# Attention and feed-forward blocks on one core: identity on VectorE, pairs of shift cells in two planes, b2 added on VectorE, a new order of instructions

## The chip, the cores and the metric

The program runs on one core of a Trainium2 chip. A core has five engines, each with its own queue that it works off in order: PE (TensorE, matrix products into PSUM), ACT (ScalarE, activation functions), DVE (VectorE), POOL (GpSimd) and SP (SyncE, which here issues all transfers between HBM and SBUF). Engines wait for each other through semaphores. The metric is the time of one execution on the device in microseconds (us), as a median of several runs.

## The reference

Two layers, each an attention block and a feed-forward block with the same weights, on a sequence of 2048 rows of width 512 in bf16; 32 heads of width 16, hidden width 1792.

```python
def _A_ref(x, wqkv, wo):
    qkv = (x @ wqkv).reshape(B, S, 3, H, Dh).transpose(2, 0, 3, 1, 4)
    q, k, v = qkv[0], qkv[1], qkv[2]
    p = softmax(einsum("bhqd,bhkd->bhqk", q, k) * Dh ** -0.5)
    o = einsum("bhqk,bhkd->bhqd", p, v)
    return o.transpose(0, 2, 1, 3).reshape(B, S, D) @ wo

def _B_ref(x, w1, b1, w2, b2):
    return gelu(x @ w1 + b1) @ w2 + b2

x = A_x
for _ in range(2):
    x = x + _A_ref(_layernorm(x), A_wqkv, A_wo)
    x = x + _B_ref(_layernorm(x), B_w1, B_b1, B_w2, B_b2)
```

## The kernel before

**Cells.** Attention is cut into cells. A cell is a 128 x 512 block of scores: 128 keys (a key tile, `kt`) against 512 columns of queries of one pass. There are 4096 cells. A cell's scores come from one matmul (`score`, L1527) into one PSUM bank; four of them with different row groups run side by side on PE. Then the exponential is taken in one of two ways.

*On ACT* (`exps`, L2120): a group of two or three cells in neighbouring banks is read at once and written as bf16 to `pt` (or to a buffer that is lent for the time: `kt`, `q`, `v`, `g`). One product with V per cell and head follows on PE (`pvs`, L2187), in rounds of four matmuls.

*On DVE and POOL, the shift cells* (`dfirst`, L1794; `dchain`, `shift`, L1983 and L1985): one `tensor_scalar` turns a score into the bits of a bf16 number near its exponential (uint16). Adding 32 to these bits three times gives four planes, and the sum of the four, with V scaled by 1, 0.84, 0.71 and 0.59 (`VC`, made by `vcopies`), is a good approximation. So a shift cell has four products on PE instead of one. Two shift cells make a pair; the additions run for both at once, as `int64_add` on POOL or, where the scheduler finds POOL too late, as `tensor_scalar` on DVE (L1985): the first from plane 0 to plane 1, the second from planes 0 and 1 together to planes 2 and 3. Planes lie in `dp` (NPL of them, each for two cells) or in parts of other tensors that are free for a time (`DU`, four planes each: `kt`, `v`). A pair takes one plane when it begins, one more for the first shift and two for the second (`grab`, `may`, `safe`); a plane comes free when its products are done (`drop`). The table `KD` names the key tiles whose cells may be shift cells; what has not been taken as such by the end of a pass goes to ACT (`next_act`).

**Banks.** PSUM has eight banks. Slot 0 of the exponentials has banks 0 to 2, slot 1 has 3 and 4, and from some time on 5 as a third (`grow`); bank 6 collects the products, bank 7, and 5 before `grow`, serve projections, feed-forward tiles and single shift cells. When a group of scores is issued, its third bank is given to a shift cell if a cell, planes and DVE's queue allow it (`trade`), else to a third cell of ACT (`more`).

**The other work.** Layer norm statistics, projections, output projection and feed-forward tiles are put between the groups of scores; weights come through four ring buffers. `init` makes the constants: a 128 x 128 identity (`IDENT`), of which the head mask (`MASK`) is a sum, rows of ones and zeros, and `B2row`, with b2 in row 0 and zeros in the others. `loads` issues the first transfers. In `ytile` the second feed-forward matmul collects 14 rounds into a bank, then a round of `ONES1` (ones in row 0) by `B2row` adds b2, and DVE adds the bank to x (L1265). In the last chunk of the last layer (four tiles) b2's round comes first. `ln` and `ln_tile` make the layer norms, the first of them behind the mask in DVE's queue. While PE would have nothing to do, it is given fillers, matmuls whose result is not used (`fill`, L1515).

**The order.** When the program is built, `_Sched` plays all threads of work against a model of the engines (costs in us at each operation, latencies, DMA tails) and so fixes the order of every queue; on the chip only semaphores count. Weights of the choices (`NAMES`, `ROWS`) change 100 times along the way, by `PIECES`.

Of the kernel before, what the change touches and what calls it, by code (L numbers as in the profile page):

```python
# [27 lines left out]
QP_RING = 3  # L28
# [5 lines left out]
XLN_RING = 4  # L34
# [12 lines left out]
NPL = 16  # L47
# [21 lines left out]
TAIL = 10  # L69
OPENING = 18  # L70
# [46 lines left out]
)  # L117
PIECES = (24, 31, 1, 10, 32, 1, 27, 27, 23, 26, 4, 5, 25, 31, 27, 29, 32, 19, 11, 28, 10, 18, 8, 13, 11, 13, 23, 13, 30, 23, 11, 9, 10, 29,
          28, 10, 16, 20, 16, 19, 14, 23, 22, 26, 31, 28, 2, 32, 8, 15, 28, 13, 28, 25, 25, 21, 13, 27, 3, 9, 29, 17, 31, 32, 28, 0, 31, 6,
          17, 31, 25, 12, 23, 28, 27, 7, 32, 22, 23, 25, 22, 9, 31, 32, 24, 32, 25, 6, 29, 30, 27, 8, 8, 11, 29, 19, 23, 25, 11, 9)  # L120
# [10 lines left out]
TTAIL = 3.2  # L131
# [7 lines left out]
SPC = 1.5  # L139
# [10 lines left out]
EARLYP = 1  # L150
# [7 lines left out]
VPER = 0.036  # L158
# [11 lines left out]
PORTS = ("OTT", "NMR", "RSTD", "RA.", "RY.", "XLN", "VC", "QP")  # L170
# [137 lines left out]
class _Sched:  # L308
# [169 lines left out]
    def run(self):  # L478
        while True:
# [71 lines left out]
            if e == "pool":  # L551
                self.pool_ops.append((start, start + cost))
# [7 lines left out]
def bass_interleave_layers__mha_block__dense_activation_gelu__prompt_kernel(  # L560
# [15 lines left out]
    with ExitStack() as es:  # L576
# [35 lines left out]
        T["DU"] += deep  # L612
        T["VC"] = sb([128, 2, 3, NKD, H // 4 * 17 + 2], BF16, "vc")
# [57 lines left out]
class _Plan:  # L671
# [12 lines left out]
    def init(self):  # L684
        T, hbm = self.T, self.hbm

        def load(dst, src, sem, keys, cost):
            return _Op("sp", cost, lambda e: e.dma_start(dst, src), writes=keys, sem=sem, by=16, tail=2.0)

        yield _Op("pool", 0.1, lambda e: e.memset(T["IDENT"][:], 0.0), writes=["IDENT"])  # L690
        yield _Op("pool", 0.3, lambda e: e.affine_select(
            out=T["IDENT"][:], in_=T["IDENT"][:], compare_op=ALU.not_equal, fill=1.0, base=0, pattern=[[-1, 128]],
            channel_multiplier=1), reads=["IDENT"], writes=["IDENT"])
        yield _Op("pool", 0.2, lambda e: e.memset(T["DP"][:, 0, 0, :].bitcast(BF16), 1.0), writes=["DP.0.0"])
        yield _Op("pool", 0.1, lambda e: e.tensor_scalar(T["ZERO"][:], T["IDENT"][:, 0:32], 0.0, None, op0=ALU.mult), reads=["IDENT"], writes=["ZERO"])
        yield _Op("pool", 0.1, lambda e: e.memset(T["ONES1"][:], 0.0), writes=["ONES1"])
        yield _Op("pool", 0.1, lambda e: e.memset(T["ONES1"][0:1, :], 1.0), reads=["ONES1"], writes=["ONES1"])
        yield _Op("pool", 0.3, lambda e: e.memset(T["B2row"][:], 0.0), writes=["B2zero"])
        yield _Op("dve", 0.6, lambda e: e.memset(self.bank(PVB), 0.0), writes=["B.%d" % PVB])
        yield _Op("dve", 0.1, lambda e: e.tensor_reduce(  # L700
            out=T["MASK"][:, :], in_=T["IDENT"][:, :].rearrange("p (a t d) -> p t a d", a=4, t=2, d=DH),
            axis=mybir.AxisListType.XY, op=ALU.add), reads=["IDENT"], writes=["MASK"])
        yield _Op("pool", 1.0, lambda e: e.memset(T["V"][0][:, :, :, 16:17], 1.0), writes=["V01"])
        z = T["ZERO"][:, 0:4].bitcast(U64)
        yield _Op("pool", 7.0, lambda e: e.int64_add(z, z, 0), reads=["ZERO"], writes=["ZERO"])

    def loads(self):
# [27 lines left out]
        yield _Op("sp", 0.2, lambda e: e.dma_start(T["B2row"][0:1, :], hbm["b2"].rearrange("(o e) -> o e", o=1)),  # L735
# [9 lines left out]
    def xmove(self, c, src, dst, sem, reads, writes):  # L745
        yield _Op("sp", 1.5, lambda e: e.dma_start(dst, src), reads=reads, writes=writes, sem=sem, by=16, tail=4.0)
# [481 lines left out]
    def ytile(self, l, seg, t):  # L1228
# [18 lines left out]
        for i, (p, key) in enumerate(row):  # L1247
# [9 lines left out]
            for j in range(2):  # L1257
                fns += self.quads(pb, T["G"][:, 2 * p + j, q], ws[j], not early and i + j == 0, early and 2 * p + j == NFC - 1)
# [669 lines left out]
    def dchain(self, pair):  # L1928
# [11 lines left out]
        if EARLYP:  # L1940
            self.products(pair, 0)
# [361 lines left out]
```

## Time and profile before

| | us |
|---|---|
| median of 3 runs | 1432.53 |
| lowest, highest | 1431.59, 1434.63 |
| the profiled execution | 1432.22 |
| its span, first to last instruction | 1430.4 |
| granted TensorE clock | 1.000 |

The page has the busy time of each engine (a matmul's end is modelled, so that PE's share says how much it had in flight, not how much it computed), groups of instructions by line, and for each group the idle time of its engine before them with what ended it. `ps` is PSUM, whichever bank; a name such as `dp` stands for all of its planes. Windows give the busy time within a stretch of the span. A bracket behind a row of the timeline names the idle time before it and its releaser; "issue" is idle time that no event in the profile explains.

### The profile page before, as it was taken

What the parts mean: (1) busy time and instruction counts of PE and PEld (TensorE: products, weight loads), DVE (VectorE), ACT (ScalarE), POOL (GpSimd) and SP (SyncE); (2) the same over time, 40 slices, a digit from 0 to 9 for tenths busy, and PEclk for the clock granted to TensorE, in tenths of its full rate; (3) what the DMA queues carried; (4) which work ended last, traced back from release to release, by engine and by line L of the source; (5) the groups of instructions that cost most, each with busy time, mean ns of one, the idle gap of its engine ahead of it and who ended that gap; (6) DMA issues with size and microseconds to landing.
All of it is one profiled execution on the core that took longest, in us unless ns stands there. A gap on an engine that the chain in (4) does not pass through costs nothing.

```text
span 1430.4 us, 45943 instructions
## 1 busy us (share of the span) xinstructions
PE 1394.1 (97%) x19566; PEld 422.3 (30%) x19566; DVE 1249.5 (87%) x2431; ACT 1395.7 (98%) x1403; POOL 988.1 (69%) x1227
## 2 busy tenths in 40 slices
PE   7999999999999999999999999999999999999999
PEld 2222222222222222222222222222222222343445
DVE  6999999979998789887899869899898887899883
ACT  5999999999999999999999999999999999999996
POOL 1378897776877677675878658657847875777581
DMA  4300001124111232213311133100113312401111
GB/s 130 79 2 2 2 2 31 38 76 96 61 46 39 75 90 68 61 38 90 105 38 39 41 103 97 54 16 2 38 34 110 90 34 87 134 18 41 30 54 55
DMA packets 122166, 80.29 MB, mean 56 GB/s; under 512 B 36717, under 2 KB 120942, under 8 KB 121966
## 3 DMA queue, kind: packets, MB, share of 16 engines
q1 hardware_dynamic: 121966, 77.36, 19.5%
q8 instruction: 157, 2.57, 0.8%
q14 instruction: 43, 0.35, 0.1%
HBM read 65.54 MB, written 4.19 MB: 49 GB/s over the span
## 4 chain that ended last, share of the span: by engine, by line
PE 51%; ACT 43%; DVE 5%; issue 1%; POOL 1%; DMA 0%; POOLq 0%; ACTq 0%
ACT pt L2120 37%; PE ps L2187 18%; PE ps L1527 17%; PE ps L681 15%; ACT kt L2120 3%; ACT g L1216 2%; DVE dp L1794 2%; PE ps L1515 1%; POOL dp L1983 0%; DVE vc L1456 0%; DVE kt L1794 0%; ACT v L2120 0%; ACT L2120 0%; ACT L1216 0%; DVE v L1794 0%
## 5 line engine op out<-in xcount | busy, mean ns | idle before, releaser
L2120 ACT ACTIVATE pt<-ps 128x1024 bf16<-128x1024 f32 (+2 forms) x1198 | 1180.2, 1114 | 4.0 <-PE ps L1527 3.0
L1983 POOL INT64_ADD dp<-dp x911 | 739.8, 820 | 291.9 <-DVE dp L1794 101.5
L1794 DVE TENSOR_SCALAR dp<-ps 128x512 uint16<-128x512 f32 x926 | 617.2, 683 | 70.1 <-PE ps L1527 65.6
L1527 PE MATMUL ps<-qp,kt 32*128 32x512 bf16 x4096 | 544.9, 384 | 12.0 <-ACT pt L2120 5.0
L2187 PE MATMUL ps<-dp,vc 128*17 128x512 bf16 (+1 forms) x3096 | 337.4, 359 | 1.9 <-POOL dp L1983 0.7
L1527 PEld LDWEIGHTS ps<-qp,kt 32*128 32x128 bf16 x4096 | 138.8, 91 | 563.9 <-ACT pt L2120 175.3
L2187 PE MATMUL ps<-pt,v 128*17 128x512 bf16 (+1 forms) x2859 | 279.8, 358 | 0.8 <-POOL kt L1983 0.5
L1983 POOL INT64_ADD kt<-kt x202 | 164.8, 819 | 77.2 <-DVE kt L1794 31.2
L1794 DVE TENSOR_SCALAR kt<-ps 128x512 uint16<-128x512 f32 x205 | 138.9, 684 | 27.9 <-PE ps L1527 27.1
L2187 PE MATMUL ps<-dp,v 128*17 128x512 bf16 (+1 forms) x1032 | 147.7, 360 | 2.2 <-DVE xt L1019 1.3
L681 PE MATMUL ps<-xf,wr 128*32 128x512 bf16 (+1 forms) x1888 | 130.2, 365 | 0.1
L2187 PE MATMUL ps<-kt,vc 128*17 128x512 bf16 (+1 forms) x777 | 118.1, 336 | 0.3 <-ACT pt L2120 0.2
L2187 PEld LDWEIGHTS ps<-dp,vc 128*17 128x17 bf16 x3096 | 89.6, 89 | 85.0 <-issue 39.9
L681 PE MATMUL ps<-wr,g 128*32 128x512 bf16 x1408 | 104.2, 383 | 2.7 <-DMA wr<-in_B_w_dram 1.5
L1983 POOL INT64_ADD v<-v x99 | 81.4, 824 | 27.0 <-DVE v L1794 8.8
L2187 PEld LDWEIGHTS ps<-pt,v 128*17 128x17 bf16 x2859 | 71.7, 88 | 78.4 <-issue 55.1
L1195 DVE TENSOR_SCALAR g<-ps,hb1t 128x512 bf16<-128x512 f32 (+1 forms) x112 | 79.2, 707 | 11.1 <-PE ps L681 11.0
L1794 DVE TENSOR_SCALAR v<-ps 128x512 uint16<-128x512 f32 x100 | 67.9, 684 | 13.6 <-PE ps L1527 12.7
L2187 PE MATMUL ps<-kt,v 128*17 128x512 bf16 (+1 forms) x401 | 73.2, 353 | 0.0
L2120 ACT ACTIVATE kt<-ps 128x1024 bf16<-128x1024 f32 (+1 forms) x68 | 69.9, 1090 | 0.2
L2187 PE MATMUL ps<-v,vc 128*17 128x512 bf16 x300 | 64.5, 381 | 0.1
L2187 PEld LDWEIGHTS ps<-dp,v 128*17 128x17 bf16 x1032 | 37.7, 88 | 35.6 <-issue 12.9
(108 smaller groups left out, 1165.5 us busy)
## 6 DMA issues: line engine op xcount, KB each, us to landing
wr<-in_B_w_dram SPq DMA_DIRECT2D x174, 256.0 KB, 3.0
wr<-in_A_wqkv_dram SPq DMA_DIRECT2D x24, 256.0 KB, 3.0
x<-in_A_x_dram SPq DMA_DIRECT2D x7, 512.0 KB, 4.3
wr<-in_A_wo_dram SPq DMA_DIRECT2D x10, 256.0 KB, 2.9
kept<-x SPq DMA_DIRECT2D x4, 512.0 KB, 2.9
x<-kept SPq DMA_DIRECT2D x4, 512.0 KB, 4.1
out_dram<-x SPq DMA_DIRECT2D x16, 128.0 KB, 1.7
q<-in_B_w_dram SPq DMA_DIRECT2D x3, 512.0 KB, 7.6
```

The lines of the kernel that those rows point to most:

```text
L681: return [lambda e, a=a: e.matmul(out[32 * a:32 * a + 32, :], lhsT=lhsT[:, 32 * a:32 * a + 32], rhs=rhs, start=start, stop=stop, tile_posi ...
L1195: yield _Op("dve", 0.21 + n / 966, lambda e, fc=fc, pb=pb: e.tensor_scalar(T["G"][:, fc, q], pb, T["HB1T"][:, fc:fc + 1], None, op0=ALU.ad ...
L1216: lambda e, g=g: e.activation(out=g, in_=g, func=ACT.Gelu_apprx_tanh), reads=gk, writes=gk, prio=2)
L1515: fns.append(lambda e, o=o, w=w, a=a, m=m: e.matmul(o, lhsT=w, rhs=rhs, start=start, stop=start, tile_position=(0, m * a)))
L1527: return (lambda e: e.matmul(o, lhsT=lhsT, rhs=rhs, start=True, stop=True, tile_position=(32 * a, 0)), ["K%d.%d.%d" % (l, gb, kt // 4), "Q ...
L1794: yield _Op("dve", 0.682, lambda e: e.tensor_scalar(u, self.bank(b), E_SCALE, E_BIAS, op0=ALU.mult, op1=ALU.add), reads=["B.%d" % b], writ ...
L1983: op = _Op("pool", PFIX + PWORD * 128 * n * (1 + both), lambda e: e.int64_add(dst, src, by * PACKED), reads=reads, writes=writes)
L2120: yield _Op("act", 0.065 + 0.4267 * n, lambda e, src=src, dst=dst: e.activation(out=dst, in_=src, func=ACT.Exp, scale=0.25), reads=["B.%d" ...
L2187: op.fns.append(lambda e, o=o, lhsT=q[0][0][m], rhs=q[0][1][:, n * m:n * m + n], a=a, st=st, sp=sp: e.matmul(o, lhsT=lhsT, rhs=rhs, start= ...
```

## The change

**Identity.** POOL's `affine_select` goes. DVE makes a row of 0 to 31 in 32 columns (a memset and five additions, doubling), transposes it in blocks of 32 x 32, and compares the two for each of the four diagonal blocks; the zeros around them are still a memset on POOL. `ZERO` is a memset, and the first `int64_add`, which has no other use than to be the first, is left out of what the scheduler holds against DVE.

**Pairs in two planes.** A pair asks for two planes (`need`). After the first shift it takes two more if they are spare (`spare`), and goes on as before. Else it waits in the scheduler until one of its cells has both of its first products issued, and the second shift is written over planes 0 and 1 (`dlate`), for each cell alone if the two belong to different passes. `NPL` goes from 16 to 17; the lent buffers are cut in halves of two planes each. `QP_RING` goes from 3 to 2 and `XLN_RING` from 4 to 3.

**b2.** `B2row` is loaded into all 128 rows by one transfer, without the memset. In all tiles but the last four, DVE adds the bank and `B2row` into an `XLN` buffer and then that to x.

**The order.** Some costs are set anew (transfers, `VPER`, the `X.` tiles among DVE's operations that are held against POOL's), `grow` begins at 240 cells instead of after all projections of layer 0, and `ROWS` and `PIECES` are new.

```diff
-QP_RING = 3
+QP_RING = 2
-XLN_RING = 4
+XLN_RING = 3
-NPL = 16
+NPL = 17
+SPARE = 0
+VCR = 2
+NEXT = 2
+GROW = 240
...
-TTAIL = 3.2
+TTAIL = 2.4
-SPC = 1.5
+SPC = 0.8
-VPER = 0.036
+VPER = 0.042
-PORTS = ("OTT", "NMR", "RSTD", "RA.", "RY.", "XLN", "VC", "QP")
+PORTS = ("X.", "OTT", "NMR", "RSTD", "RA.", "RY.", "XLN", "VC", "QP")
...
-        yield _Op("pool", 0.3, lambda e: e.affine_select(
-            out=T["IDENT"][:], in_=T["IDENT"][:], compare_op=ALU.not_equal, fill=1.0, base=0, pattern=[[-1, 128]],
-            channel_multiplier=1), reads=["IDENT"], writes=["IDENT"])
-        yield _Op("pool", 0.3, lambda e: e.memset(T["B2row"][:], 0.0), writes=["B2zero"])
+        yield small(lambda e: e.memset(iota[:, 0:1], 0.0), [], ik)
+        for i in range(5):
+            w = 1 << i
+            yield small(lambda e, w=w: e.tensor_scalar(iota[:, w:2 * w], iota[:, 0:w], float(w), None, op0=ALU.add), ik, ik)
+        yield small(lambda e: e.transpose(rows, iota), ik, rk)
+        for i in range(4):
+            p = slice(32 * i, 32 * i + 32)
+            yield small(lambda e, p=p: e.tensor_tensor(out=T["IDENT"][p, p], in0=iota[p, :], in1=rows[p, :], op=ALU.is_equal),
+                        ik + rk + ["IDENT"] * (i == 0), ["IDENT"] if i == 3 else ["IDENT.%d" % i])
...
-            if i == last and not early:
-                fns += self.quads(pb, T["ONES1"][:, :], T["B2row"][:, :], False, True)
...
+        if early:
+            yield _Op("dve", DV, lambda e: e.tensor_tensor(out=x, in0=x, in1=pb, op=ALU.add), reads=["B.%d" % b, xk], writes=[xk])
+            yield ("rel", "misc", b)
+        else:
+            r = yield ("acq", "xln")
+            yb, yk = T["XLN"][:, r, :], "XLN.%d" % r
+            yield _Op("dve", DV, lambda e: e.tensor_tensor(out=yb, in0=T["B2row"][:, :], in1=pb, op=ALU.add),
+                      reads=["B.%d" % b, "B2row"], writes=[yk])
+            yield ("rel", "misc", b)
+            yield _Op("dve", 0.151 + 0.267, lambda e: e.tensor_tensor(out=x, in0=x, in1=yb, op=ALU.add), reads=[yk, xk], writes=[xk], prio=EVAC)
+            yield ("rel", "xln", r)
...
-            pair["need"] = 4
+            pair["need"] = 2
...
         if own:
-            yield ("cond", lambda: self.may(pair, 2))
-            self.grab(pair, 2)
+            yield ("cond", lambda: self.spare(pair) or any(pair["seen"]))
+            if not any(pair["seen"]) or self.spare(pair):
+                self.grab(pair, 2)
...
+        parts = [(0, n)] if n == 1 or cells[0][0] == cells[1][0] else [(0, 1), (1, 2)]
+        for part in parts:
+            self.s.spawn(self.dlate(pair, *part), CPRIO)
...
+    def spare(self, pair):
+        free = len(self.s.pools["pl"]) - 2
+        if free < SPARE:
+            return False
...
+        return self.safe(free, todo)
+
+    def dlate(self, pair, lo, hi):
+        yield ("cond", lambda: all(pair["seen"][j] == 2 for j in range(lo, hi)))
+        key = [self.dkey(pair, i, j) for i in range(2) for j in range(lo, hi)]
+        yield self.shift(pair, 0, 0, (lo, hi), True, 2, key, key, self.s.clock["pool"] <= self.s.clock["dve"] + PMORE)
+        for i in range(2, 4):
+            self.products(pair, i, lo, hi)
```

More of the change, by code (lines that the diff above doesn't have):

```diff
@@ L700, in init, with small @@
-        yield _Op("dve", 0.1, lambda e: e.tensor_reduce(
+        iota, rows = T["OTT"][:, 0, 0:32], T["OTT"][:, 1, 0:32]
+        ik, rk = ["OTT.0.0", "OTT.0.1"], ["OTT.1.0", "OTT.1.1"]
+        def small(fn, reads, writes, cost=0.15):
+            op = _Op("dve", cost, fn, reads=reads, writes=writes, prio=0)
+            op.port = False
+            return op
+        yield _Op("pool", 0.15, lambda e: e.memset(T["IDENT"][:], 0.0), writes=["IDENT"])
+        yield small(lambda e: e.memset(iota[:, 0:1], 0.0), [], ik)
@@ L1438, in vcopies @@
         T = self.T
-        first, used = {}, [None, None]
+        first, used = {}, [None] * VCR
         for pi, v in enumerate(self.visit):
@@ L1859, in over @@
     def over(self, du):
-        return self.deep[du - self.own] if du >= self.own else []
+        return self.deep[(du - self.own) // 2] if du >= self.own else []
     def vone(self, l, kt):
@@ L1970, in dchain @@
+        out = 2 if len(pair["pl"]) == 4 else 0
+        if out:
+            new = [self.dkey(pair, i, j) for i in (2, 3) for j in range(n)]
+            yield self.shift(pair, 0, 2, (0, n), True, 2, key[0] + key[1], new, self.s.clock["pool"] <= self.s.clock["dve"] + PMORE)
             for p in pair["pl"][:2]:
@@ L1972, in dchain, with shift @@
                     yield ("rel", "pl", p)
[L1973 to L1977 removed]
+            for i in range(2, 4):
+                self.products(pair, i)
+            return
+        parts = [(0, n)] if n == 1 or cells[0][0] == cells[1][0] else [(0, 1), (1, 2)]
[5 more added lines that the diff above has]
+            return False
+        todo = []
+        for x in self.active:
+            ps = [c[0] for c in x["cells"]]
+            hi = max(ps) if x is not self.open else self.pa + 1
+            todo.append([min(ps), hi, x["need"], x["held"] + (2 if x is pair else 0)])
+        return self.safe(free, todo)
[3 more added lines that the diff above has]
+        yield self.shift(pair, 0, 0, (lo, hi), True, 2, key, key, self.s.clock["pool"] <= self.s.clock["dve"] + PMORE)
+        for i in range(2, 4):
+            self.products(pair, i, lo, hi)
+    def shift(self, pair, i, o, part, both, by, reads, writes, pool):
+        lo, hi = part
+        n = hi - lo
+        src, dst = self.planes(pair, i, hi, both, lo), self.planes(pair, o, hi, both, lo)
         if pool:
```

163 lines of the change are left out of this document (78 added, 85 removed), and 10 rows, old and new, of the table ROWS.

## The prediction

> **What bounds the kernel now.** I read the page first, then the busy time by windows, then the start in order of time, then the groups by form.
>
> ```profile
> span 1430.4 us, 45943 instructions
> PE 1394.1 (97%) x19566; PEld 422.3 (30%) x19566; DVE 1249.5 (87%) x2431; ACT 1395.7 (98%) x1403; POOL 988.1 (69%) x1227
> ```
>
> PE and ACT are both over 97% busy, DVE has 1430.4 − 1249.5 = 180.9 us to spare and POOL 442.3. ACT's busy time in three windows (columns: window, length, busy and count, clock, DMA) says where its 2% are:
>
> ```profile
> 0.00:21.00 21.00, 3.71 (x6) 1.00 0.60 178
> 21.00:1404.00 1383.00, 1379.73 (x1378) 1.00 0.20 55
> 1404.00:1431.00 27.00, 12.23 (x20) 1.00 0.14 41
> ```
>
> Between 21 and 1404 us ACT lacks 3.3 us. The time is therefore a start of 21, ACT's own work of 1383, and a tail of 27 in which PE closes the last tiles. It changes only if ACT begins sooner, has less to do, or is made to wait. The start, in order of time:
>
> ```profile
> 0.74 1.82 SPq L711 DMA_DIRECT2D x<-in_A_x_dram  x4
> 0.92 0.48 DVE L699 MEMSET ps<- 128x512 f32 x1 [0.92 <-PEq L2288]
> 8.48 0.28 POOL L691 TENSOR_SCALAR_AFFINE_SELECT ident<-ident 128x128 bf16<-128x128 bf16 x1 [7.55 <-issue]
> 8.80 0.28 DVE L700 TENSOR_REDUCE mask<-ident 128x2 f32<-128x128 bf16 x1 [7.39 <-POOL ident L691]
> 9.00 0.68 DVE L791 BATCH_NORM_STATS2 stats<-x 128x6 f32<-128x512 bf16 x1
> 13.03 0.30 DVE L803 TENSOR_SCALAR ry<-varr 128x2 int32<-128x2 int32 x2
> 14.42 0.28 DVE L812 SCALAR_TENSOR_TENSOR nmr<-mv,rstd 128x2 f32<-128x2 f32 x2
> 21.19 2.37 ACT L2120 ACTIVATE pt<-ps 128x1536 bf16<-128x1536 f32 x2 [1.72 <-PE ps L1527]
> x<-in_A_x_dram SPq DMA_DIRECT2D x4, 128.0 KB, 2.3
> ```
>
> POOL sits 7.55 us before its first select, which no instruction explains ("issue"). The mask waits 7.39 us for it, and the first layer norm statistics stand behind the mask in DVE's queue, although the first tile of x, issued at 0.74 with a median of 2.3 us to landing, is there at about 3.0.
>
> ACT's work by form, with the four small groups of three-cell exponentials:
>
> ```profile
> L2120 ACT ACTIVATE pt<-ps 128x1024 bf16<-128x1024 f32 x1038 | 979.3, 1058 | 1.8 <-PE ps L1527 1.0
> L2120 ACT ACTIVATE pt<-ps 128x1536 bf16<-128x1536 f32 x159 | 228.2, 1479 | 2.2 <-PE ps L1527 2.0
> L2120 ACT ACTIVATE kt<-ps 128x1536 bf16<-128x1536 f32 x6 | 8.9, 1479 | 0.0
> L2120 ACT ACTIVATE v<-ps 128x1536 bf16<-128x1536 f32 x6 | 8.6, 1454 | 0.1
> L2120 ACT ACTIVATE q<-ps 128x1536 bf16<-128x1536 f32 x2 | 3.0, 1490 | 0.0
> L2120 ACT ACTIVATE g<-ps 128x1536 bf16<-128x1536 f32 x1 | 1.4, 1446 | 0.0
> ```
>
> A group that carries a third cell costs ACT 1479 − 1058 = 421 ns more. 159 + 6 + 6 + 2 + 1 = 174 groups do; in the others the third bank goes to a shift cell on DVE, or to nothing. So a cell moved to DVE is worth 0.421 us.
>
> **The identity.** It replaces POOL's select by eleven small DVE operations (a memset, five additions, a transpose, four comparisons). Dependent small operations follow each other at (14.42 − 13.03) / 7 = 0.20 us, so eleven take 2.2. DVE begins at 0.92, then 0.48 for the bank and 0.28 for the mask: statistics from 3.9 instead of 9.00, so **−5.1 us**. Bounds: if the eleven cost nothing, x's landing at 3.0 still holds it (−6.0); I put −3 at the other end, for landings beyond the median. What is late next is the weights: issued from 2.60 with at most 5.7 us to landing, they are not.
>
> ```profile
> 2.60 2.63 SPq L711 DMA_DIRECT2D g<-in_A_wqkv_dram  x5
> g<-in_A_wqkv_dram SPq DMA_DIRECT2D x2, 384.0 KB, 5.7
> ```
>
> The last is there by 2.60 + 2.63 + 5.7 = 10.9, and the first exponential at 21.19 − 5.1 = 16.1. POOL's remaining load of the integer add is over long before the first shift. On what an unexplained wait before a first POOL instruction is, the Trainium skill's GPSIMD Engine Reference, "Instruction dispatch", says that the first call to freshly loaded code pays about 6 us with no instruction shown; the 7.55 us here agree roughly, and by the page the wait moves to the integer add and is not saved on POOL, which costs nothing as long as no shift is due.
>
> **b2.** For 28 of 32 tiles the one-round matmul of ones and b2 goes (the last four tiles keep theirs), and DVE adds b2 while it evacuates, then adds the result to x.
>
> ```profile
> L681 PE MATMUL ps<-b2row,ones 128*32 128x512 bf16 x128 | 12.3, 379 | 0.0
> 1421.09 2.76 PE L681 MATMUL ps<-q,g 128*32 128x512 bf16 x48
> 1420.87 0.39 PE L681 MATMUL ps<-b2row,ones 128*32 128x512 bf16 x4
> L822 DVE TENSOR_SCALAR xln<-x,rstd,nmr 128x512 bf16<-128x512 bf16 x64 | 25.4, 420 | 0.3
> L1015 DVE TENSOR_TENSOR v<-v,ps 128x512 f32<-128x512 f32 x16 | 10.9, 678 | 0.6 <-PE ps L2187 0.5
> ```
>
> Four matmuls make a round; 48 in 2.76 against 4 in 0.39 makes (2.76 − 0.39) / 11 = 0.215 us a round. PE is rid of 28 × 0.215 = 6.0 us. DVE's first add stays one pass over the bank; the second has no row, so it lies between the 420 ns of a 512-wide pass in bf16 and the 678 of an add with a bank. I take 0.42, since both its operands are bf16 in SBUF: 28 × 0.42 = 11.8 us (at most 19.0), out of 180.9 idle. Were that cover gone it would be 11.8 us of DVE, but not of ACT. x is ready 0.4 us later per tile, for a layer norm that no exponential waits for at once.
>
> **The pairs.** A pair of shift cells now asks for two planes instead of four; its second shift writes over the first two planes once PE has used them, unless two planes are spare. With 17 planes for 16, eight pairs may be open instead of four, so fewer third banks go to ACT for want of planes. How many cells are there to move?
>
> ```profile
> L1794 DVE TENSOR_SCALAR dp<-ps 128x512 uint16<-128x512 f32 x926 | 617.2, 683 | 70.1 <-PE ps L1527 65.6
> L1794 DVE TENSOR_SCALAR kt<-ps 128x512 uint16<-128x512 f32 x205 | 138.9, 684 | 27.9 <-PE ps L1527 27.1
> L1794 DVE TENSOR_SCALAR v<-ps 128x512 uint16<-128x512 f32 x100 | 67.9, 684 | 13.6 <-PE ps L1527 12.7
> L1515 PE MATMUL ps<-b2row 128*32 128x512 bf16 x448 | 36.0, 384 | 0.2 <-DVE dp L1794 0.2
> L1515 PE MATMUL ps<-b2row,zero 128*17 128x512 bf16 x52 | 5.1, 385 | 0.0
> ```
>
> 926 + 205 + 100 = 1231 cells are on DVE. The table KD, which stays, names 1320 of the 4096. So 89 at most can move: 37.5 us of ACT. PE sets a second limit. A moved cell has four products instead of one, three matmuls more, 0.75 × 0.215 = 0.16 us. What PE has to spare is at least its fillers, matmuls that no result needs: (448 + 52) / 4 = 125 rounds, 26.9 us. With b2's 6.0, and the span shrinking by 0.421 a cell, n cells fit while 0.58 n < 32.9: 56 cells, 23.7 us. The count lies between 0 and 56. I take **37**, where the cells cost PE what b2 gives back (37 × 0.16 = 6.0), so that only the shorter span eats into the fillers: 37 × 0.421 = **−15.6 us**. On DVE they cost 37 × 0.684 = 25.3, on POOL about 37 × 0.82 = 30.3 by its shift's mean; both fit.
>
> ```profile
> POOL dp L1983 <- PE ps L2187: 49.9, 32, 8.2
> L1983 POOL INT64_ADD dp<-dp x911 | 739.8, 820 | 291.9 <-DVE dp L1794 101.5 <-PE ps L2187 49.9 <-DVE vc L1456 25.6
> ```
>
> **The rest.** The DMA times, the port list and the new rows of weights change no instruction, only the order in which the kernel's scheduler puts them; I give them 0. GROW lends bank 5 to the exponentials from 240 cells on, which leaves one bank for the projections until they are done. 18 of them fall in that stretch:
>
> ```profile
> L935 DVE CAST q<-ps 128x512 bf16<-128x512 f32 x12 | 8.1, 677 | 0.0
> L935 DVE CAST kt<-ps 128x512 bf16<-128x512 f32 x6 | 4.0, 668 | 0.0
> ```
>
> If each waits for the one before, 12.1 us at most; if none is due, 0, which I take, since ACT has its queue full throughout. The smaller rings for QP and XLN make writers wait on DVE at worst, where 180.9 us are idle.
>
> **The sum.** 1430.4 − 5.1 − 15.6 = 1409.7 for the span. The profiled execution took 1432.22, 1.8 beyond its span, and the median of the runs is 1432.53, 0.3 above that: **1412 us**.
>
> **The rivals.**
> *Only the start is kept.* Planes were not what lacked, the cells stay 1231: 1432.5 − 5.1 = 1427.4. For it: POOL's shifts waited for planes still in use only 32 times. Against it: 174 groups took a third cell.
> *PE is no limit.* All 89 cells move: 1432.5 − 5.1 − 37.5 = 1389.9. For it speaks PEld's 30%, against it that PE fills only 26.9 us. The Trainium skill's Perfetto Trace Analysis, "Identifying the Most-Contended Engine", says that matmul busy time tells little and LDWEIGHTS share more; by that rule this rival would hold.
> *Slower: POOL waits in place.* The in-place shift must wait until PE has used both planes, and POOL's queue is in order: behind it stand the first shifts of other pairs, and PE's products wait for those. A wait for PE costs 49.9 / 32 = 1.56 us. dp holds 926 / 2 = 463 pairs; if a share s waits so, POOL loses 722 s, and it has 442.3: it decides from s = 0.61. At s = 0.75 the excess is 99 us; at (2 × 0.82 + 1.56) / 2 = 1.6 us a cell POOL sheds 62 cells, which return to ACT for 26.1: 1432.5 − 5.1 + 26.1 = 1453. Against it: the order is made so that shifts come after their products, and spare planes avoid the wait.
> *The identity does not help*, because something else holds the start (a late tile of x): 1432.5 − 15.6 = 1417.
>
> **How the numbers follow.** Forecast 0.52; only the start 0.20; PE no limit 0.07; POOL waits 0.14; no help at the start 0.07. Low end: 1432.5 − 6.0 − 23.7 = 1403, and half way on towards the 89 cells, 1399. High end: the start alone at its lower bound, −3: 1430, which also holds the forecast with GROW's 12.1. About 0.2 lie outside. Within 0.2% (2.9 us, about what a measurement of this kernel can tell from no change) is 0.05: a small start gain, or a little of POOL's waits. Slower 0.12, the rest of that rival; faster 0.83.
>
> **What would show it.** Statistics of the first tile near 3.9 us and the first exponential near 16.1. The three L1794 groups (renumbered) at 1268 together, three-cell exponentials near 137. No b2 matmul but 16, and 28 short adds near 0.42 us. POOL waiting for PE more often than 32 times, yet under 442 us in total. The forecast is wrong if ACT has gaps between its start and its tail beyond 3.3 us, or if the cells on DVE stay at 1231 or fall.

## The result, and the profile after

| | before | after |
|---|---|---|
| median, us; before with the runs made beside the change | 1433.05 (1431.59 to 1434.63) | 1421.13 (1420.57 to 1423.24), 4 runs |
| ratio to before, 95% interval | 1 | 0.9919 [0.9902, 0.9937] |
| span of the profiled execution | 1430.4 | 1419.1 |
| granted TensorE clock | 1.000 | 1.000 |
| first exponential | 21.19 | 15.68 |
| first exponential to the last load of the gelu table on ACT | 1382.75 | 1377.01 |

The changed kernel is 0.8% faster. The forecast was 1412 us; the gain is 11.9 us instead of 20.5. In the two spans 5.51 us come from the start, 5.74 from the long stretch between the first exponential and the last gelu table load, and 0.05 from the tail. The busy line of the page after:

```profile
PE 1387.4 (98%) x19432; PEld 417.4 (29%) x19432; DVE 1268.7 (89%) x2498; ACT 1390.4 (98%) x1392; POOL 974.3 (69%) x1221
```

ACT by windows (window, length, busy and count, clock, DMA), cut where its start and its tail are now:

```profile
0.00:15.60 15.60, 3.71 (x6) 1.00 0.69 209
15.60:1393.00 1377.40, 1374.73 (x1367) 1.00 0.20 55
1393.00:1420.00 27.00, 11.98 (x20) 1.00 0.10 32
```

In the middle ACT lacks 2.7 us of being busy throughout (3.3 before). Read alone, that says again that ACT paces the stretch. What such a row hides is worked out below from the start times. The start, in order of time:

```profile
0.90 3.59 DVE L701 TENSOR_SCALAR ott<-ott 128x1 bf16<-128x1 bf16 x5
...
1.80 2.25 POOL L715 MEMSET v<- 128x512 bf16 x1
3.87 0.19 POOL L717 INT64_ADD zero<-zero  x1
...
6.36 0.68 DVE L803 BATCH_NORM_STATS2 stats<-x 128x6 f32<-128x512 bf16 x1
...
15.68 1.45 ACT L2165 ACTIVATE pt<-ps 128x1536 bf16<-128x1536 f32 x1 [1.27 <-PE ps L1547]
```

The first statistics start at 6.36, not at the 3.9 that was forecast: the five additions alone took 3.59 us, 0.72 each. The first exponential is nevertheless where it was forecast (16.1), because the way from the first statistics to it shrank by 2.87 us, from 21.19 − 9.00 = 12.19 to 15.68 − 6.36 = 9.32. Before, one small operation in that chain ran beside a long memset of POOL and took 1.47 us, against 0.17 for the same operation on the next tiles; now no memset is left beside the chain. That explains at most 1.3 of the 2.87. The rows of before:

```profile
10.39 2.26 POOL L703 MEMSET v<- 128x512 bf16 x1
...
11.21 1.47 DVE L801 TENSOR_SCALAR varr<-mv 128x2 f32<-128x2 f32 x1
...
12.95 0.17 DVE L801 TENSOR_SCALAR varr<-mv 128x2 f32<-128x2 f32 x1
```

ACT by form, the shift cells, b2, the fillers and POOL's waits, after:

```profile
L2165 ACT ACTIVATE pt<-ps 128x1024 bf16<-128x1024 f32 x1005 | 950.6, 1057 | 1.8 <-PE ps L1547 0.9
L2165 ACT ACTIVATE pt<-ps 128x1536 bf16<-128x1536 f32 x176 | 253.4, 1497 | 1.3 <-PE ps L1547 1.3
...
L2165 ACT ACTIVATE v<-ps 128x1536 bf16<-128x1536 f32 x4 | 5.8, 1462 | 0.0
...
L2165 ACT ACTIVATE kt<-ps 128x1536 bf16<-128x1536 f32 x3 | 4.4, 1480 | 0.0
L2165 ACT ACTIVATE q<-ps 128x1536 bf16<-128x1536 f32 x2 | 3.0, 1483 | 0.0
L2165 ACT ACTIVATE g<-ps 128x1536 bf16<-128x1536 f32 x2 | 3.0, 1476 | 0.0
```

```profile
L1814 DVE TENSOR_SCALAR dp<-ps 128x512 uint16<-128x512 f32 x846 | 563.9, 681 | 59.3 <-PE ps L1547 53.8 <-POOL dp L2028 1.3
...
L1814 DVE TENSOR_SCALAR kt<-ps 128x512 uint16<-128x512 f32 x265 | 179.2, 684 | 29.3 <-PE ps L1547 27.6
...
L1814 DVE TENSOR_SCALAR v<-ps 128x512 uint16<-128x512 f32 x128 | 86.6, 684 | 9.8 <-PE ps L1547 9.2
...
L1535 PE MATMUL ps<-b2row 128*32 128x512 bf16 x500 | 40.2, 384 | 0.3 <-DVE v L962 0.2
...
L1283 DVE TENSOR_TENSOR xln<-b2row,ps 128x512 bf16<-128x512 bf16 x28 | 18.9, 676 | 1.4 <-PE ps L680 1.3
L1286 DVE TENSOR_TENSOR x<-x,xln 128x512 bf16<-128x512 bf16 x28 | 12.1, 433 | 0.1
...
L1535 PE MATMUL ps<-b2row,zero 128*17 128x512 bf16 x40 | 3.9, 383 | 0.0
...
L680 PE MATMUL ps<-b2row,ones 128*32 128x512 bf16 x16 | 1.4, 379 | 0.0
```

```profile
POOL dp L2028 <- PE ps L2232: 29.8, 17, 5.2
```

Shift cells: 846 + 265 + 128 = 1239, eight more than before, not 37. Three-cell groups: 176 + 4 + 3 + 2 + 2 = 187, more than the 174 of before, not fewer. The fillers rose from 500 matmuls to 540. b2 went as written: 16 of its matmuls are left, and the short add takes 433 ns. POOL waits for PE less than before on `dp`, 17 times and 29.8 us against 32 and 49.9.

The first row of ACT also shows what the windows hide: 1005 exponentials of 1.057 us are busy for only 950.6 us together, so that neighbours overlap by some 0.11 us. A wait shorter than this overlap leaves no gap. By the start times in the trace, an exponential of two cells is followed by the next instruction after 0.904 us at the least, half of them within 0.905, a tenth after 0.98 or more; one of three cells after 1.330. Against these shortest distances ACT's exponentials lose 27.0 us in the changed kernel and 28.7 in the kernel before, where the windows show 2.7 and 3.3. 20.4 us of the 27.0 and 22.6 of the 28.7 end with a score matmul of PE. This loss, "by start times", is used below.

### The profile page after: what moved, and what is told of

It reads as the page before. It is cut to its first block, busy times and chain, and to the rows that moved or that the text cites. A ratio compares the mean times of both kernels' runs of the same rounds, so it can differ in the third digit from the quotient of the medians.

```text
span 1419.1 us, 45762 instructions
## 1 busy us (share of the span) xinstructions
PE 1387.4 (98%) x19432; PEld 417.4 (29%) x19432; DVE 1268.7 (89%) x2498; ACT 1390.4 (98%) x1392; POOL 974.3 (69%) x1221
## 4 chain that ended last, share of the span: by engine, by line
PE 48%; ACT 42%; DVE 8%; POOL 1%; DMA 1%; issue 1%; POOLq 0%; DVEq 0%
ACT pt L2165 35%; PE ps L2232 17%; PE ps L1547 16%; PE ps L680 14%; DVE dp L1814 2%; ACT kt L2165 2%; ACT q L2165 2%; ACT v L2165 1%; ACT g L1229 1%; DVE kt L1814 1%; POOL dp L2028 1%; DVE v L1814 1%; PE ps L1535 1%; DVE stats L803 1%; DMA wr<-in_B_w_dram 1%
## 5 line engine op out<-in xcount | busy, mean ns | idle before, releaser
L2165 ACT ACTIVATE pt<-ps 128x1024 bf16<-128x1024 f32 (+1 forms) x1181 | 1171.4, 1122 | 3.1 <-PE ps L1547 2.1
L2028 POOL INT64_ADD dp<-dp x829 | 670.8, 819 | 245.3 <-DVE qp L1495 52.6
L1814 DVE TENSOR_SCALAR dp<-ps 128x512 uint16<-128x512 f32 x846 | 563.9, 681 | 59.3 <-PE ps L1547 53.8
L2232 PE MATMUL ps<-dp,vc 128*17 128x512 bf16 (+1 forms) x2832 | 304.8, 359 | 1.6 <-POOL v L2028 0.4
L2028 POOL INT64_ADD kt<-kt x255 | 204.7, 807 | 114.3 <-DVE kt L1814 48.9
L1814 DVE TENSOR_SCALAR kt<-ps 128x512 uint16<-128x512 f32 x265 | 179.2, 684 | 29.3 <-PE ps L1547 27.6
L2232 PE MATMUL ps<-dp,v 128*17 128x512 bf16 (+1 forms) x944 | 136.6, 359 | 3.5 <-DVE xt L1031 2.6
L2028 POOL INT64_ADD v<-v x124 | 99.5, 807 | 53.2 <-DVE v L1814 25.7
L1814 DVE TENSOR_SCALAR v<-ps 128x512 uint16<-128x512 f32 x128 | 86.6, 684 | 9.8 <-PE ps L1547 9.2
L2232 PEld LDWEIGHTS ps<-pt,v 128*17 128x17 bf16 x2835 | 70.4, 88 | 80.7 <-issue 55.8
L2165 ACT ACTIVATE v<-ps 128x1024 bf16<-128x1024 f32 (+1 forms) x50 | 50.5, 1084 | 0.1
```

The source lines that it names most:

```text
L1814: yield _Op("dve", 0.682, lambda e: e.tensor_scalar(u, self.bank(b), E_SCALE, E_BIAS, op0=ALU.mult, op1=ALU.add), reads=["B.%d" % b], writ ...
L2028: op = _Op("pool", PFIX + PWORD * 128 * n * (1 + both), lambda e: e.int64_add(dst, src, by * PACKED), reads=reads, writes=writes)
L2165: yield _Op("act", 0.065 + 0.4267 * n, lambda e, src=src, dst=dst: e.activation(out=dst, in_=src, func=ACT.Exp, scale=0.25), reads=["B.%d" ...
L2232: op.fns.append(lambda e, o=o, lhsT=q[0][0][m], rhs=q[0][1][:, n * m:n * m + n], a=a, st=st, sp=sp: e.matmul(o, lhsT=lhsT, rhs=rhs, start= ...
```

## The experiments

Each ratio is to the kernel before, measured beside it; the changed kernel's is 0.9919 [0.9902, 0.9937]. The intervals of experiments 5, 9, 10 and 11 overlap this one, so that their medians alone tell no difference. Between two kernels the stretch from the first exponential to the last gelu table load is therefore compared, in one profiled execution each. It leaves out the start, which itself varied by up to 1.3 us among kernels with the changed start as it is (15.47 to 16.80).

**1. The identity alone, in the order of before.** DVE's identity in place of POOL's select, with `ZERO` as a memset; nothing else.

```diff
-        yield _Op("pool", 0.3, lambda e: e.affine_select(...), reads=["IDENT"], writes=["IDENT"])
+        yield small(lambda e: e.memset(iota[:, 0:1], 0.0), [], ik)
...
```

> The kernel before, with the identity made on VectorE as in the change; every queue keeps its order but for the first microseconds (two fillers fewer). If the start's gain is carried through to the end, the first exponential moves from 21.19 to about 15.7 us and the time falls by as much: 1433.0 - 5.5 = 1427.5. Rival: something later (weights, PE) paces the early stage, and the gain is lost on the way: the first exponential still comes early, but the time stays at 1433.

1428.98 us, ratio 0.9967 [0.9955, 0.9980], 4.7 us less than its before. The first exponential:

```profile
16.97 3.71 ACT L2134 ACTIVATE pt<-ps 128x1536 bf16<-128x1536 f32 x3 [1.73 <-PE ps L1541]
```

It is 4.22 us sooner, and the stretch behind it is 1398.99 − 16.97 = 1382.02, 0.7 less than before: in that order what the start gains is kept to the end. The first statistics start at 6.62 here, so that the way from them to the first exponential is 10.35 us. Of the 2.87 us by which it shrank, 1.84 came with the identity and 1.03 with the new order.

**2. b2's rounds alone left out, in the order of before.** 28 output tiles lack b2.

```diff
-                fns += self.quads(pb, T["ONES1"][:, :], T["B2row"][:, :], False, True)
+                fns[-4:] = self.quads(pb, T["G"][:, 2 * p + 1, q], ws[1], False, True)
```

> The kernel before without the 28 rounds that add b2 on PE (the output lacks b2 in these tiles); all queues keep their order. If PE's queue is in the way wherever it works, 28 x 0.215 us go: 1433.0 - 6.0 = 1427.0. Rival: ACT paces the whole stretch and PE's rounds are hidden behind it: 1433, within 1 us.

1431.08 us, 0.9982 [0.9973, 0.9991]: 2.6 us of the 6.0 by which PE has less to do. So PE is partly in the way of ACT in the kernel before. ACT's loss by start times falls by 3.0, from 28.7 to 25.7 us.

**3. 28 rounds given back to PE in the changed kernel**, matmuls with zero weights, in the same tiles and order.

```diff
+            if i == last and not early:
+                fns[:0] = [lambda e, a=a: e.matmul(pb[32 * a:32 * a + 32, :], lhsT=T["ZERO"][:, 0:32], rhs=T["B2row"][:, :], ...) for a in range(4)]
```

> The changed kernel with 28 rounds put back on PE, one per tile where b2's stood (their weights are zero, so that they add nothing); DVE's work and all orders stay. If PE's queue is in the way: 1421.1 + 6.0 = 1427.1. Rival: hidden behind ACT, 1421, within 1 us.

1427.55 us, 0.9959 [0.9947, 0.9972].

```profile
16.53 2.37 ACT L2169 ACTIVATE pt<-ps 128x1536 bf16<-128x1536 f32 x2 [1.24 <-PE ps L1551]
...
1398.74 1.28 ACT L1229 ACT_TABLE_LOAD   x1
```

The same last row in the changed kernel:

```profile
1392.69 1.28 ACT L1229 ACT_TABLE_LOAD   x1
```

The stretch grows from 1392.69 − 15.68 = 1377.01 to 1398.74 − 16.53 = 1382.21, 5.2 us or 0.19 a round: nearly the 0.215 us of a round. PE has no slack where these rounds stand, though ACT is "busy" for 98% of the span; ACT's loss by start times rises from 27.0 to 32.2 us. The Trainium skill's Perfetto Trace Analysis, "Identifying the Most-Contended Engine", would judge PE's headroom by its FLOPs and the share of LDWEIGHTS instead of matmul time; that share is 29% here, and PE was in the way all the same.

**4. Less work for ACT everywhere.** All exponentials into buffers already written once read 464 of 512 columns; the rest of those cells keeps old values.

```diff
+            w = 464 if all(r in seen for r in run) else 512
...
-            yield _Op("act", 0.065 + 0.4267 * n, lambda e, src=src, dst=dst: e.activation(
+            yield _Op("act", 0.065 + 0.4267 * n, lambda e, src=src[:, :, 0:w], dst=dst[:, :, 0:w]: e.activation(
```

> The changed kernel with ACT's exponentials cut to 464 of 512 columns wherever a buffer has been written before (the rest of the buffer keeps old values); all orders stay. A third cell of 512 columns costs 1497 - 1057 = 440 ns, so 48 columns are 41 ns a cell, some 115 us of ACT's work over about 2800 cells. If ACT alone paces, PE follows until its fillers (540 matmuls, 135 rounds, 29 us) are used up: 1392 or below. Rival: PE's queue is as full as ACT's although it has fillers, and the time falls by less than 10 us.

1415.12 us, 0.9872 [0.9859, 0.9886]: 6 us less, of some 115 by the columns. What ACT waits for, in this kernel and, behind it, in the changed one (in total, times, longest):

```profile
ACT pt L2167 <- PE ps L1547: 19.1, 60, 1.2
```

```profile
ACT pt L2165 <- PE ps L1547: 2.1, 4, 1.3
```

These gaps are a small part of it. ACT's busy time falls by 55.8 us (1390.4 to 1334.6), because exponentials that wait no longer overlap. By start times ACT's loss rises from 27.0 to 130.7 us, and 126.9 of that ends with a score matmul. For 98 of these 127 us, no weight load of PE had waited for another engine in the microsecond before the matmul; for 27 one had waited for DVE or POOL. So PE's own queue is the main part of what holds ACT back here, and DVE and POOL behind it a smaller one. No run gave DVE less to do.

**5. The third cell left out of every fifth three-cell group.** Its scores are still made, its exponential isn't, so its output is old data.

```diff
+            cut = n == 3 and three % 5 == 0 and run[2] in seen
...
+            k = 2 if cut else n
+            yield _Op("act", 0.065 + 0.4267 * n, lambda e, src=src[:, 0:k, :], dst=dst[:, 0:k, :]: e.activation(
```

> The changed kernel, but in every fifth of the 187 three-cell groups, 37 in all, ACT leaves the third cell out (its buffer keeps old values, and PE uses them); all orders stay. It is what 37 moved cells take off ACT, without what they add elsewhere. By the prediction's price 37 x 0.421 = 15.6 us go: 1421.1 to 1405.5. Rival: PE's queue does not follow, because it is nearly as full as ACT's in these places: 5 us or less.

1419.49 us, 0.9908 [0.9891, 0.9926], 1.6 us less; the stretch is 1390.68 − 15.48 = 1375.20, 1.8 less. The large form of `pt` fell from 176 to 142:

```profile
L2169 ACT ACTIVATE pt<-ps 128x1536 bf16<-128x1536 f32 x142 | 204.7, 1475 | 2.5 <-PE ps L1547 1.9
```

With one more among those of the other buffers 35 third cells are left out, 14.7 us by 0.421 us each. The stretch gained 1.8, so 88% of that came back as waits: ACT's loss by start times rises from 27.0 to 40.1 us, and 33.3 of that ends with a score matmul. One case can be read off the timeline: nine exponentials in a row, in the changed kernel and then in this one, where one of two three-cell groups among the nine has lost its third cell (such a row merges both forms under the first one's).

```profile
303.29 9.21 ACT L2165 ACTIVATE pt<-ps 128x1024 bf16<-128x1024 f32 x9
```

```profile
303.03 5.12 ACT L2169 ACTIVATE pt<-ps 128x1024 bf16<-128x1024 f32 x5
308.54 3.77 ACT L2169 ACTIVATE pt<-ps 128x1024 bf16<-128x1024 f32 x4 [0.40 <-PE ps L1547]
```

Nine took 9.21 us; now they take 308.54 + 3.77 − 303.03 = 9.28. ACT runs ahead by a third cell and then stands for 0.40 us until PE has the next scores.

**6. Are the fillers what PE has to spare?** All fillers that use `B2row` write 16 columns instead of 512.

```diff
+            n = 16 if src == ["B2row"] else 512
-            fns.append(lambda e, o=o, w=w, a=a, m=m: e.matmul(o, lhsT=w, rhs=rhs, ...))
+            fns.append(lambda e, o=o[:, 0:n], w=w, a=a, m=m, rhs=rhs[:, 0:n]: e.matmul(o, lhsT=w, rhs=rhs, ...))
```

> The changed kernel with its fillers cut from 512 to 16 columns (all but the first ones, before PE has real work); all orders stay. If fillers only use time in which PE would wait, the time stays at 1421.1 within 1.5 us, and PE's 29 us in them are spare, as the prediction took them. Rival: fillers hold up the scores behind them, and the time falls by several us. A lower granted clock would show in the profile and make it longer.

1432.77 us, 0.9999 [0.9988, 1.0010]: 11.6 us slower than the changed kernel. The granted clock fell (clock behind the busy time):

```profile
core 0: 1429.6 us, clock 0.986
...
800.00:1000.00 200.00, 185.70 (x2468) 0.96 0.20 56
1000.00:1200.00 200.00, 195.17 (x2557) 0.97 0.22 62
```

So whether time freed from fillers could be used isn't answered by this run. It shows only that this time can't be left empty without cost; products of moved cells in place of the fillers would fill it.

**7 and 8. The planes by themselves.** The 100 chosen rows of weights belong to one kernel each, so both kinds of pairs were run with the same single row of weights: with the two planes of the change, and with the four of before (with its `NPL`, `QP_RING` and `XLN_RING`).

```diff
-ROWS = (...)
-PIECES = (10, 12, 14, 25, 19, ...)
+ROWS = ((0.5, 0.3, 0.8, 0.2, 18, 10, 2, 6, 1, 1, 2, 2, 5, 1.4, 9.5, 2, 3.5, 24, 3, 4, 0.4, 1.0, 0, 1, 1, 3, 1, 2, 0.3, 2, 0.3, 0.0, 0.35),)
+PIECES = (0, 0, 0, ...)
```

> The changed kernel with one row of weights from start to end in place of the 100 chosen ones. It is the pair to the next run: there the pairs of cells take four planes as before (16 planes, rings of 3 and 4), all else being equal. If planes are what lacks, this run has some 35 shift cells more than the next and is 35 x 0.421 = 15 us faster. Rival: more shift cells, but about the same time, since what a moved cell takes off ACT it puts on PE and on DVE. Both should be slower than 1421, for the order's part in the result: 1430 to 1460.

> The pair to the run before: the changed kernel with one row of weights all along and with the pairs of cells as they were before, four planes each. If planes are what lacks: 15 us above the run before. Rival: within 4 us of it, with fewer shift cells.

Two planes: 1452.06 us, 1.0138 [1.0122, 1.0154]. Four planes: 1451.57 us, 1.0131 [1.0113, 1.0149]. ACT's share of the busy line, its waits for scores, and the two longest of them; two planes first:

```profile
PE 1400.7 (97%) x19432; PEld 417.3 (29%) x19432; DVE 1247.9 (86%) x2454; ACT 1402.2 (97%) x1405; POOL 977.7 (67%) x1217
...
ACT pt L2133 <- PE ps L1515: 18.9, 15, 9.4
...
749.45 11.11 ACT L2133 ACTIVATE pt<-ps 128x1024 bf16<-128x1024 f32 x12 [9.37 <-PE ps L1515]
...
909.68 5.61 ACT L2133 ACTIVATE pt<-ps 128x1024 bf16<-128x1024 f32 x6 [3.90 <-PE ps L1515]
```

```profile
PE 1403.4 (97%) x19465; PEld 421.2 (29%) x19465; DVE 1225.2 (84%) x2409; ACT 1417.0 (98%) x1395; POOL 958.2 (66%) x1184
...
ACT pt L2105 <- PE ps L1515: 4.4, 12, 1.2
```

Two planes bring 1217 shift cells against 1181: 36 more, almost the 37 of the forecast. ACT's busy time is 14.8 us less, close to 36 × 0.421 = 15.2. Yet the spans are 1449.3 and 1450.1, 0.8 us apart, and the intervals of the two ratios overlap: ACT's waits for scores rose by 14.5. But two stalls, of 9.37 and 3.90 us, are 13.3 of these; the kernel with four planes has none above 1.2. So the planes do what they say, and the equal time is not made of many small waits. Whether the two planes cause the two stalls, or this one row of weights happens to, no run tells. This pair therefore doesn't settle what a moved cell is worth. Both kernels stand some 20 us above before: the 100 chosen rows are worth about 31 us against this one row (1452.06 − 1421.13). What the new rows are worth against those of before is not shown.

**9 and 10. A round less on PE, alone and with the third cells.** Each of the 28 tiles leaves out one round of its second feed-forward product; then the same together with experiment 5.

```diff
-                fns += self.quads(pb, T["G"][:, 2 * p + j, q], ws[j], not early and i + j == 0, i == last and j == 1)
+                if early or i != 1 or j == 0:
+                    fns += self.quads(pb, T["G"][:, 2 * p + j, q], ws[j], not early and i + j == 0, i == last and j == 1)
```

> The changed kernel, in which each of the 28 late feed-forward tiles leaves out one of its rounds of four matmuls in the second feed-forward product (28 rounds, as many as b2 took before), so that the output lacks that part; order unchanged. If PE's queue alone paces the stretch, the time falls by about what 28 more rounds cost, 6.4 us, to 1414.7 us. If ACT alone paces it, nothing: 1421. If the two limit by turns (the present theory), between them: about -3 us, 1418.

> The changed kernel with both cuts: the 28 left-out rounds on PE and, on ACT, the third cell left out of 37 three-cell exponentials (15.6 us of ACT's time by 0.421 us each), so that the output lacks both; order unchanged. The third cells alone gave -1.6 us. If the cuts are independent, the gains add: the sum of the two runs' gains, about -5 us, 1416. If PE and ACT stand side by side as limits (the present theory), each cut alone is stopped by the other engine and together they give more than their sum: -7 us or more, 1414 or less.

Alone: 1420.50 us, 0.9914 [0.9900, 0.9927], and the stretch is 1392.68 − 15.48 = 1377.20: nothing. Both: 1418.50 us, 0.9898 [0.9885, 0.9912], stretch 1390.51 − 16.51 = 1374.00, 3.0 us less. Here both expectations missed. The gain of both is not much more than the sum. 28 rounds more cost 5.2 us in experiment 3, and 28 rounds fewer give 0 here. They don't stand at one place, though: the added round comes before a tile's last two, the round left out is its fourth of 14. So the two runs show places where PE has no slack and places where ACT doesn't wait for it, and not that PE and ACT are even to within a round at one of them. In experiment 10 the two cuts don't lie at the same groups either, which may be why they don't help each other; experiment 12 tries that.

**11. POOL's memsets behind the identity.** The first memset after the zeros of `IDENT` waits for the identity, so that the others come later too.

```diff
-        yield _Op("pool", 0.4, lambda e: e.memset(T["DP"][:, 0, 0, :].bitcast(BF16), 1.0), writes=["DP.0.0"])
...
+        yield _Op("pool", 0.4, lambda e: e.memset(T["DP"][:, 0, 0, :].bitcast(BF16), 1.0), reads=["IDENT"], writes=["DP.0.0"])
```

> The changed kernel with its POOL memsets put behind the identity (the first of them, ones for the normalizer's columns, now waits for it), two of the warm-up fillers gone with it; everything after the start in the same order. If the five small DVE instructions took 691 ns each because POOL's memsets ran beside them, they take some 0.2 us now, the first statistics start near 4 us instead of 6.36, the first exponential up to 2.5 us sooner (near 13.2 us), and the time is about 1418.7 us. If they are slow of themselves, or x lands later than that, nothing moves: 1421, or the memsets, now later, delay the first V tiles and it is slower by up to 2 us.

1420.73 us, 0.9915 [0.9901, 0.9928]. The start, in order of time:

```profile
0.90 0.98 DVE L701 TENSOR_SCALAR ott<-ott 128x1 bf16<-128x1 bf16 x5
...
3.74 0.69 DVE L803 BATCH_NORM_STATS2 stats<-x 128x6 f32<-128x512 bf16 x1
...
13.08 2.36 ACT L2165 ACTIVATE pt<-ps 128x1536 bf16<-128x1536 f32 x2 [1.27 <-PE ps L1547]
```

The same five additions take 0.98 us, 0.20 each, once no memset runs beside them, against 3.59; so POOL's memsets made them slow. The Trainium skill's SBUF — State Buffer, "SBUF: two separate sides", says that DVE and GpSimd share a pair of ports, and that a GpSimd instruction, or a DVE one of certain kinds, locks it for its whole length; the two starts, 3.59 and 0.98 us, agree with that. The first exponential comes 2.60 us sooner than in the changed kernel. But the median moves by 0.4. The loads of ACT's tables, which stand at the same points of both orders, show where the gain goes; the changed kernel first:

```profile
302.00 1.28 ACT L2165 ACT_TABLE_LOAD   x1
...
469.44 1.28 ACT L2165 ACT_TABLE_LOAD   x1
```

```profile
299.68 1.28 ACT L2165 ACT_TABLE_LOAD   x1
...
468.65 1.28 ACT L2165 ACT_TABLE_LOAD   x1
```

It is 2.32 us ahead at 302 and 0.79 at 469, and at the next such load, at 641, 0.13. Most of the first loss falls at 316 us. For the weights' ring from 308 to 316 us (idle time of PE and of its weight loads until a piece had landed, and how long the pieces took), the changed kernel and then this one:

```profile
  DMA wr<-in_B_w_dram: 0.2, 1
...
DMA to landing us min/median/max: 2.6/3.3/3.9
```

```profile
  DMA wr<-in_B_w_dram: 3.4, 4
...
DMA to landing us min/median/max: 4.3/5.2/5.5
```

PE asks for the weights earlier and they take longer to land, so that they are there at much the same time. The second loss, at 476 us, looks alike: PE's idle time for `wr` between 465 and 478 us is 2.1 us instead of 0.6, and the median landing 5.0 instead of 4.1. Why these loads took longer was not tried. At these two places it is the weights' landing that takes back a faster start.

**12. Both queues relieved at the same places.** The third cells of experiment 5, and in those groups and the next ones score matmuls of 16 columns.

```diff
+            w = 16 if self.group.get(cell) in self.cuts else 512
+            return e.matmul(o[:, 0:w], lhsT=lhsT, rhs=rhs[:, 0:w], start=True, stop=True, tile_position=(32 * a, 0))
...
+            if cut:
+                self.cuts |= {u, u + 1}
```

> The changed kernel with the third cell left out of some 35 three-cell exponentials, as in the run that gained 1.6 us, and at the same places PE relieved too: the score matmuls of that group and of the next (70 groups, 225 cells) write 16 columns instead of 512, so that the output lacks these. Order unchanged. ACT is spared 35 x 0.421 = 14.7 us as before; PE some 70 x 0.2 = 14 us in the same groups. If PE's queue is what gives the third cells' time back right behind each of them (the present theory), both now gain at once: -8 to -14 us against the changed kernel, 1407 to 1413. If something else holds the groups back (DVE's evacuations, the waits between the engines, the loads), it stays near the third cells' own -1.6: 1418 to 1420.

1414.79 us, 0.9867 [0.9851, 0.9884]; the stretch is 1386.25 − 16.59 = 1369.66, 7.35 us less than in the changed kernel and 5.5 less than with the third cells alone. The median gain, 6.3 us, falls short of the 8 that was expected at least; 0.9 us of that is this run's late first exponential (16.59 against 15.68). The nine exponentials of experiment 5:

```profile
303.91 8.81 ACT L2179 ACTIVATE pt<-ps 128x1024 bf16<-128x1024 f32 x9
```

They took 8.81 us instead of 9.21, in one piece: the 0.40 is kept, because PE is no longer late behind it. Over the whole stretch half of the 14.7 us is kept. The other half still comes back as waits for PE: ACT's loss by start times is 34.5 us, against 27.0 in the changed kernel and 40.1 with the third cells alone, and 28.8 of it ends with a score matmul. PE's relief alone at these places was not run, so it isn't shown how much of the 5.5 us it would give by itself. Nor is it shown whether it's the work spared in PE's queue or the earlier end of the short scores.

## Why the prediction was right or wrong

**Direction and range: right, in part by luck.** 1421 lies in the range, and faster was the likely case. But of the sum's two terms only the start came as forecast; the stretch gave 5.7 us of 15.6, and not all of that from moved cells.

**What bounds the kernel: half right.** The prediction took ACT's busy time in the middle for ACT's own work, with 3.3 us lacking. By start times ACT lost 28.7 us there, and 22.6 of that ended with PE's scores. So PE was already a second limit, as experiment 2 shows too.

**The start, −5.1: right in size, wrong in its way.** Experiment 1 gave 4.7, the changed kernel 5.5. But eleven small operations at 0.20 us were priced by rows in which nothing of POOL ran; the first five ran beside POOL's memsets at 0.72. That cost 2.5 us of the forecast's statistics at 3.9; without these memsets, in experiment 11, they started at 3.74. 2.9 came back on the way from the statistics to the first exponential: 1.84 with the identity, of which a clash with a memset that I had not read, in the 1.47 us row of before, is at most 1.3; and 1.03 with the new order. Two errors cancelled, and that is luck. The 5.7 us to landing of the weights, read as the most, is a median; the longest of these loads took 6.0, which changes nothing.

**The remark on POOL's wait: not confirmed.** That the unexplained 7.55 us would move to the integer add, as the prediction read the Trainium skill's GPSIMD Engine Reference, "Instruction dispatch", did not happen: L717 ran at 3.87 right behind a memset, in 0.19 us.

**b2, 6.0 us off PE: right in what it does**, and DVE's price (0.42 forecast, 0.433 measured) too. As time of its own it was put at nothing; alone it was worth 2.6 us, and in the new order as many rounds put back cost 5.2.

**The pairs, 37 × 0.421 = −15.6: this step failed.** Its number was wrong: 8 cells moved, 3.4 us by the same price. The bound from PE's fillers said that up to 56 fit. With one row of weights for both kinds of pairs it was 36, so that the planes do allow the number; the small count came with the new rows of weights, which the profile of before couldn't show. Why they left it at 8 stays open. The price is right as what a third cell costs ACT (1.330 − 0.904 = 0.426 by start times), but it is not what the kernel gets where ACT alone is relieved: experiments 4 and 5 show that PE's scores for the next group come when they come, and ACT then waits. Whether 37 moved cells would have brought 15.6 us was not tested in the new order. The sentence behind the step, that PE has at least its fillers to spare, did not hold where it was tested: 28 rounds, 6.0 us by the forecast's own measure and far below the 26.9, cost 5.2.

**The rest, 0.** The new order was given nothing. The stretch fell by 5.74. By start times 4.0 of it is less work for ACT: the eight cells, and eleven groups fewer at 0.05 us each beside their cells. 1.7 is shorter waits. b2's rounds shorten waits (experiment 2), and the new order fills PE's rounds of products better: zero-weight matmuls that fill up such rounds (L2195 before, L2240 after) fell from 115 to 43. No run separates the two.

**The rivals.** *Only the start is kept* (1427) is the nearest to what the cells did, yet 6 us more came. *PE no limit* fell with experiment 3. *POOL waits in place* fell: POOL waited for PE less than before on `dp`. *No help at the start* fell with experiment 1. The sign by which I would have known the failure, cells near 1231, is what came (1239); the other, gaps on ACT beyond 3.3 us, is not: they are 2.7. That sign was blind, since most of ACT's waits are shorter than the overlap of its exponentials.

## What to carry to other kernels

A busy share of 98% on one engine neither says that this engine alone paces nor that it hardly waits: where its instructions overlap in the profile, count from start to start. If a second queue is nearly even with it, work taken from the first can come back as a wait a few instructions later (13 of 15 us in experiment 5), and relief of both at the same places keeps more of it (half in experiment 12). Test it from both sides, by giving a round back and by taking one away at the same place, before a moved piece of work is priced at its full duration. Where the order of queues was chosen for one kernel, compare parts of a change under one and the same order; and before an equal time is read as no effect, look whether a few long stalls make it.

## What the runs showed of the hardware

- Short fillers cost clock: with the fillers at 16 columns the granted TensorE clock was 0.96 and 0.97 between 800 and 1200 us and 0.986 on the mean, against 1.000, and the run took 11.6 us more.
- Neighbouring exponentials on ACT overlap in the profile: of two cells (1024 columns) each lasts 1.017 us or more in the changed kernel, and the next instruction starts 0.904 us after it at the least; of three cells the distance is 1.330. A busy row therefore hides waits of some 0.1 us.
- A DVE addition of a few columns took 0.72 us beside POOL's memsets and 0.20 without them; in the layer norm a small operation took 1.47 beside another memset, and 0.17 on the next tiles.
- POOL's integer add ran with no wait at 3.87 us in the changed kernel, while in the kernel before POOL stood 7.55 us before its select and 5.49 before the add. The change took a select and a `tensor_scalar` off POOL and moved the add forward, and both waits are gone; which of these did it isn't shown. The add of before:

```profile
18.14 0.18 POOL L705 INT64_ADD zero<-zero  x1 [5.49 <-issue]
```
